# Turning round the branch to a second path, with branch hints ahead of it, at the end of an attention and feed-forward kernel

## The chip, the cores and the metric

The kernel runs on one core of one Trainium2 chip. The metric is the device time of one execution in microseconds (us). Three runs of the kernel before took 246.99, 247.65 and 247.90 us, median 247.65. A further execution was profiled: it took 247.33 us, and its span, from the first to the last instruction of the program, is 244.8 us (244.82 in the trace).

A core has five engines with a sequencer each: TensorE (PE; its weight loads are listed as PEld), VectorE (DVE), ScalarE (ACT), GpSimd (POOL) and SyncE (SP). Each runs its own list of instructions, and they wait for each other by semaphores.

## The reference

Attention in chunks of 64 rows, then a gated feed-forward layer without a nonlinearity:

```
q, k, v: (8, 8, 576, 64)            chunks of 64 along the 576
scores = q_c @ k_c^T / sqrt(64);  scores -= rowmax(scores)
attn   = exp(scores) / (rowsum + 1e-9);  a = attn @ v_c
x      = a as (4608, 512)           rows: batch and position, columns: heads
out    = ((x @ w1) * (x @ w2)) @ w3 @ w_out        w1, w2: (512, 1024), w3: (1024, 1024), w_out: (1024, 512)
```

## The kernel before

The 4608 rows are cut into 18 pieces of 256 (`p` below), two of which form a group. For each piece, GpSimd's queue loads q, k and v; VectorE transposes q and k (`do_T`); TensorE makes the scores (`do_S`), ScalarE their exponentials without subtracting the row maximum (`do_E`), TensorE the product with v and a column of ones (`do_P`), VectorE divides by the sums (`do_N`) and transposes (`do_X`). For each group and each 128 columns of the hidden layer, TensorE makes x @ w1 and x @ w2 (`do_A`, `do_B`), ScalarE copies the first out (`do_C`) and VectorE multiplies the two (`do_M`). The product w3 @ w_out is made once on the chip (`do_V`, `do_W`, `do_Z`), so that one more product per piece gives the output (`do_O`); ScalarE copies it out of PSUM (`do_Y`, line 382) and SyncE's queue stores it (`do_Q`, line 200). The last piece, `O17`, is stored in three parts, each after a copy of its own (line 375): two copies on ScalarE, the last on VectorE.

The order of all this is written out by hand in `ORDER`: a step's letter names the function, its numbers the piece and the part. Each engine executes its instructions in that order.

Since the exponentials are taken without the row maximum, their sums may leave the range in which the result can be trusted. Step `F` (`do_F`) tests the stored reciprocals of the sums and writes to `flag` how many of the 128 partitions are sound. Step `L` (`do_L`, line 428) loads `flag` into a register of each engine. It stands near the end of `ORDER`:

```
... O15 Y14 Q14 L O16 Y15 Q15 Y16 Q16 O17
```

When all steps have been issued, line 507 opens a conditional block: if fewer than 128 partitions are sound, the whole computation is done again by a second path, `do_rescue`, which subtracts the row maximum. With the inputs of the reference all partitions are sound, and the second path is not executed.

How the branch is laid out matters here. The program has these blocks: the main part, which ends with a compare-and-branch on each of the five engines; the second path; an *even-out* block, which is executed when the second path is not, and brings the semaphores to the values that they would have behind the second path (one to five semaphore instructions per engine); and the end, with the drains and a barrier of all engines (its instructions carry line 534). In the kernel before, the blocks lie in this order on each engine: main part, even-out block, second path, end. The compare-and-branch falls through into the even-out block, and the even-out block ends with a jump over the second path to the end; the profile lists both as COMPARE_BRANCH of line 507. Counted in the program, the second path is 7523 instructions long on TensorE, 281 on VectorE, 192 on ScalarE, 187 on GpSimd and 1 on SyncE; the main part has 5560, 287, 204, 149 and 139.

SyncE's part of the end waits for the landing of every store that is still under way, and then reports to the barrier like the others. GpSimd collects the reports.

Of the kernel before, what the change touches and what calls it, by code (L numbers as in the profile page):

```python
# [44 lines left out]
def kernel(  # L45
# [13 lines left out]
    P = 128  # L59
# [365 lines left out]
    whole = []  # L425

    def do_L():
        whole.append(nc.values_load(flag[:], min_val=0, max_val=P))

    def do_rescue():  # L430

# [72 lines left out]
          "W": do_W, "Z": do_Z, "O": do_O, "Y": do_Y, "Q": do_Q, "F": do_F, "L": do_L}  # L504
    for step in ORDER.split():
        do[step[0]](*(int(n) for n in step[1:].split(".") if n))
    with tc.If(whole[0] < P, preferred_fallthrough_block=False):  # L507
        do_rescue()


# [28 lines left out]
```

## Time and profile before

| what | us |
|---|---|
| median of three runs | 247.65 (246.99 to 247.90) |
| the profiled execution | 247.33 |
| its span | 244.8 |
| TensorE busy | 225.6 (92%) |
| VectorE busy | 155.4 (63%) |
| ScalarE busy | 85.0 (35%) |
| GpSimd busy | 83.2 (34%) |
| mean granted TensorE clock | 0.994 of full speed |

The page of the profile gives busy time per engine, the span in 40 slices, the DMA queues, the chain of waits that ended last, and the groups of instructions by line. Register, branch, semaphore and DMA-issuing instructions are not counted as busy; they are found by asking the trace for one line of the program. There, an engine's sequencer is written with a q (PEldq, DVEq). Among the DMA queues, the page lists two of the kind "instruction": q8 with 23 packets and 0.38 MB, so about 16 KB each, and q14 with 11 packets and 0.09 MB, about 8 KB each. These carry the engines' own instructions. The stores run on q1.

### The profile page before, as it was taken

What the parts mean: (1) busy time and instruction counts of PE and PEld (TensorE: products, weight loads), DVE (VectorE), ACT (ScalarE), POOL (GpSimd) and SP (SyncE); (2) the same over time, 40 slices, a digit from 0 to 9 for tenths busy, and PEclk for the clock granted to TensorE, in tenths of its full rate; (3) what the DMA queues carried; (4) which work ended last, traced back from release to release, by engine and by line L of the source; (5) the groups of instructions that cost most, each with busy time, mean ns of one, the idle gap of its engine ahead of it and who ended that gap; (6) DMA issues with size and microseconds to landing.
All of it is one profiled execution on the core that took longest, in us unless ns stands there. A gap on an engine that the chain in (4) does not pass through costs nothing. (4 is left out here: it accounts for less than half of the span.)

```text
span 244.8 us, 6384 instructions
## 1 busy us (share of the span) xinstructions
PE 225.6 (92%) x2731; PEld 120.1 (49%) x2753; DVE 155.4 (63%) x238; ACT 85.0 (35%) x116; POOL 83.2 (34%) x112
## 2 busy tenths in 40 slices
PE   1289989999999989999999999999999999999991
PEld 1247878864545444444444444444444444444450
DVE  1756799699799588999998899647450431242000
ACT  2412424423334335335135263243223332423240
POOL 8847876556985336754050410000000000000000
PEclk9999999999999999999999999999999999999997
DMA  7999999999999999999999794555202201200434
GB/s 178 179 185 179 185 168 202 196 192 169 163 174 226 228 210 263 185 214 198 219 209 271 161 156 115 133 153 193 64 1 90 85 0 69 105 1 0 171 122 145
DMA packets 93746, 37.71 MB, mean 154 GB/s; under 512 B 75152, under 2 KB 86672, under 8 KB 93712
## 3 DMA queue, kind: packets, MB, share of 16 engines
q0 software_dynamic: 82592, 18.88, 83.1%
q1 hardware_dynamic: 10080, 17.83, 24.1%
q10 hardware_dynamic: 1040, 0.52, 0.8%
q8 instruction: 23, 0.38, 0.6%
q14 instruction: 11, 0.09, 0.1%
HBM read 38.80 MB, written 9.44 MB: 197 GB/s over the span
## 5 line engine op out<-in xcount | busy, mean ns | idle before, releaser
L93 PE MATMUL ab_ps<-xt,w 128*128 128x512 bf16 (+1 forms) x681 | 127.0, 342 | 1.0 <-DVE xt L283 0.3
L93 PEld LDWEIGHTS <-w 128*128 128x128 bf16 x704 | 67.1, 98 | 55.4 <-issue 1.3
L352 DVE TENSOR_TENSOR ab<-a_sb,ab_ps 128x512 bf16<-128x512 f32 x71 | 47.6, 674 | 40.5 <-ACT a_sb L337 40.1
L337 ACT COPY a_sb<-ab_ps 128x512 f32<-128x512 f32 x71 | 41.6, 586 | 81.3 <-PE ab_ps L93 81.1
L93 PE MATMUL o_ps<-w3o,ab 128*128 128x512 bf16 (+1 forms) x285 | 63.3, 373 | 0.6
L208 DVE STREAM_TRANSPOSE qkT<-qk 128x1024 bf16<-128x1024 bf16 x36 | 45.0, 1287 | 7.2 <-ACT qk L143 5.6
L93 PEld LDWEIGHTS <-ab 128*128 128x128 bf16 x296 | 28.4, 98 | 32.3
L96 POOL DMA_DIRECT2D vbuf<-in_v_dram x40 | 33.9, 854 | 17.6 <-DMA qk<-in_k_dram 5.0
L382 ACT COPY o_sb<-o_ps 128x1024 f32<-128x1024 f32 x17 | 17.2, 1012 | 45.5 <-PE o_ps L93 41.3
L271 DVE TENSOR_TENSOR xn<-pv,rcs 128x512 bf16<-128x512 f32 x36 | 24.9, 691 | 1.4
L96 POOL DMA_DIRECT2D qk<-in_q_dram x23 | 18.1, 789 | 9.0 <-DVE ab L352 2.6
L96 POOL DMA_DIRECT2D qk<-in_k_dram x23 | 18.0, 786 | 8.1 <-DMA vbuf<-in_v_dram 5.3
L241 ACT ACTIVATE e<-s_ps 128x1024 bf16<-128x1024 f32 x16 | 15.9, 1028 | 1.9 <-PE s_ps L93 1.8
L93 PE MATMUL w_ps<-wo,w3T 128*128 128x512 bf16 x62 | 13.9, 379 | 0.1
L291 DVE STREAM_TRANSPOSE xm<-xn 128x512 bf16<-128x512 bf16 x20 | 13.6, 697 | 0.2
L268 DVE RECIPROCAL rcs<-pv 128x8 f32<-128x8 f32 x36 | 6.9, 193 | 10.4 <-PE pv L93 10.4
L96 POOL DMA_DIRECT2D w<-in_moe_w_dram x16 | 11.1, 696 | 5.6 <-DMA wo<-in_moe_w_out_dram 2.9
L93 PEld LDWEIGHTS <-e 64*32 64x32 bf16 (+1 forms) x832 | 7.8, 97 | 8.9 <-issue 7.1
L93 PE MATMUL pv<-vbuf,e 64*32 64x65 bf16 (+1 forms) x832 | 10.2, 198 | 1.9 <-ACT e L241 1.1
L283 DVE STREAM_TRANSPOSE xt<-xn 128x512 bf16<-128x512 bf16 x16 | 11.4, 711 | 0.5
L93 PEld LDWEIGHTS <-qkT 32*64 32x64 bf16 x512 | 5.6, 117 | 10.5 <-DVE qkT L208 8.1
L375 DVE COPY o_sb<-o_ps 128x256 f32<-128x256 f32 x1 | 0.4, 425 | 16.0 <-PEq L507 16.0
(30 smaller groups left out, 54.5 us busy)
## 6 DMA issues: line engine op xcount, KB each, us to landing
out_dram<-o_sb SPq DMA_DIRECT2D x17, 512.0 KB, 4.0
qkm<-qkT SPq DMA_DIRECT2D x40, 128.0 KB, 4.9
vbuf<-in_v_dram POOLq DMA_DIRECT2D x32, 128.0 KB, 8.5
w<-in_moe_w_dram POOLq DMA_DIRECT2D x16, 256.0 KB, 9.6
qk<-in_q_dram POOLq DMA_DIRECT2D x11, 256.0 KB, 7.1
qk<-in_k_dram POOLq DMA_DIRECT2D x11, 256.0 KB, 7.7
xt<-xm SPq DMA_DIRECT2D x40, 64.0 KB, 3.0
wo<-in_moe_w_out_dram POOLq DMA_DIRECT2D x4, 256.0 KB, 7.5
```

The lines of the kernel that those rows point to most:

```text
L93: return inorder(nc.tensor.matmul(*a, **kw))
L96: return inorder(nc.gpsimd.dma_start(dst, src))
L208: inorder(nc.vector.transpose(qkT_t[g][:, :, p % 2, s, heads(h)].rearrange("p e h (y t) -> p h t e y", t=2), qk_t[p][:, s, heads(h)].rearr ...
L241: inorder(nc.scalar.activation(e_t[p][:, :, heads(hh)], s_t[p][:].rearrange("p u (h q) -> p u h q", q=CH)[:, :, heads(hh)], Exp, scale=sca ...
L268: inorder(nc.vector.reciprocal(rc, pv[:, :, :, D:W]))
L271: inorder(nc.vector.tensor_mul(xn_t[p][:, u], pv[:, :, :, 0:D], rc.to_broadcast([P, 2, 4, D])))
L283: inorder(nc.vector.transpose(new_xt(g)[:].rearrange("p (o t) -> p o t", o=KO)[:, :, t0:t0 + UT] .rearrange("p o (m y) -> p m o y", y=BL), ...
L291: inorder(nc.vector.transpose(xm_t[g][:, u, :, m].rearrange("p o (c y) -> p c o y", y=BL), xn_t[p][:].rearrange("p u r m d -> p (u r) m d" ...
L337: inorder(nc.scalar.copy(a_t[p, j][:], ps_t[p, j][:, 0, :]))
L352: inorder(nc.vector.tensor_mul(o, view(a_t.pop((p, j))[:]), view(ps_t.pop((p, j))[:, 1, :])))
L375: inorder(copy(o_sb[:, u, n0:n1], t[:, 0, 0:n1 - n0]))
L382: inorder(nc.scalar.copy(o_sb[:], ps_t.pop(p)[:]))
```

## The change

```diff
     def do_L():
         whole.append(nc.values_load(flag[:], min_val=0, max_val=P))
+        tc.mark_branch_hint_location("whole", "LikelyTaken",
+                                     (mybir.EngineType.PE, mybir.EngineType.DVE, mybir.EngineType.Activation))
...
-    with tc.If(whole[0] < P, preferred_fallthrough_block=False):
+    with tc.If(whole[0] < P, preferred_fallthrough_block=True, label="whole"):
         do_rescue()
```

It has two parts. With `preferred_fallthrough_block=True` the compare-and-branch falls through into the second path and branches to the even-out block, which now lies behind the second path, next to the end: main part, second path, even-out block, end. The jump from the even-out block to the end is no longer needed. And on TensorE, VectorE and ScalarE a hint instruction is placed at step `L`, behind the load of the register: it names the branch with the label `whole` and says that it will likely be taken. GpSimd and SyncE get no hint. Nothing of the computation is changed or moved.

## The prediction

> **What bounds the kernel now.** I read the page first: TensorE is busy in 92% of the span, and it is still at full share in the last slices, so up to about 239.6 us the matmuls set the time and the change touches none of them. The page's chain of waits says nothing of the rest: it holds one copy.
>
> ```profile
> ## 4 chain that ended last, share of the span: by engine, by line
> DVE 0%
> DVE o_sb L375 0%
> ```
>
> That copy ends at 240.1, and the span ends at 244.8. So 4.7 us at the end hold no counted work, and only sequencer instructions can say what fills them. Next I asked for the instructions of line 507 (the branch) from 236 us on. Columns: instruction, count, shortest/median/longest duration in ns, first and last start in us.
>
> ```profile
> L507 PEldq COMPARE_BRANCH  x2: 91/2084/4077, 237.3 to 239.8; - x2
> L507 ACTq COMPARE_BRANCH  x2: 38/42/45, 238.8 to 239.2; - x2
> L507 DVEq COMPARE_BRANCH  x2: 51/53/55, 239.7 to 240.2; - x2
> L507 SPq COMPARE_BRANCH  x2: 38/46/53, 240.5 to 240.6; - x2
> ```
>
> Each engine branches twice: the test, which falls through to the even-out block, and a jump from there over the second path to the end. TensorE's jump, at 239.78, takes 4.08 us. The drains behind the jumps (line 534, from 239.6 to 244 us) show who arrives when:
>
> ```profile
> L534 ACTq DRAIN  x1: 81/81/81, 239.7 to 239.7; - x1
> L534 DVEq DRAIN  x1: 58/58/58, 243.5 to 243.5; - x1
> L534 PEldq DRAIN  x1: 75/75/75, 243.9 to 243.9; - x1
> ```
>
> ScalarE loses 0.4 us in its jump, VectorE 3.2 (240.24 to 243.48), TensorE 4.1. The DMA view of 241.3 to 241.5 us says why: a packet of the instruction queue q8 begins at 241.34 and takes 1.09 us, and a q14 packet of 8 KB begins at 241.51. The target's instructions have to be brought in.
>
> ```profile
> q1 hardware_dynamic: 36, 0.02, 38.6%
> q8 instruction: 1, 0.02, 34.2%
> ```
>
> The third thing at the end is the last store, as SyncE's waits show (total us, times, longest):
>
> ```profile
> SPq L534 <- DMA out_dram<-o_sb: 2.2, 1, 2.2
> ```
>
> It is issued at 240.13. Of its 16 semaphore increments in the trace, 15 come from 241.66 to 242.01 (median 241.74), the last at 243.57. The DMA view of 242.5 to 244 us has 8 late packets of 1 KB in it, one DMA engine's part, which start when the q8 packet ends:
>
> ```profile
> q1 hardware_dynamic: 8, 0.01, 2.4%
> ```
>
> So TensorE's fetch also holds up the last store. SyncE reports 0.21 us after the landing (243.78), TensorE at 244.00, and the two closing barrier rounds take 0.82 us from there to 244.82. The store alone would end the span at 244.6. **Only the fetch's removal from both places shortens the span.**
>
> **Part 1, turning the branch.** It removes one jump per engine: the even-out block now lies next to the end. The test becomes the far jump. TensorE's sequencer reads the test at 237.27, 2.3 us before its last matmul ends, so a stall there is partly covered: 237.36 + 4.08 = 241.4 instead of 243.9. On VectorE the test is read at 239.71, beside the copy; with a stall of 3.24, even-out (0.1) and drain it would report at 243.13 instead of 243.5. GpSimd's branch is at 181.5 and it reports with the drain of 185.0: nobody waits for it. SyncE saves one branch (0.1 us) ahead of its 2.2 us wait: nothing.
>
> **Part 2, the hints.** One instruction each on TensorE, VectorE and ScalarE behind the register load of line 428. No row shows a hint. Below: it costs no more than a branch that does not stall, 0.04 to 0.09 us. Above: its sequencer stands for a whole fetch, 4.08 us. At the load (228.6) TensorE's sequencer is about 4.1 us ahead of its array (the group it has finished handing over ends only at 232.7, where ScalarE's copy starts), so 0.5 us at most would show; VectorE is idle for 16 us there, ScalarE for 2.9 us. I take the lower end: the register load at the same place takes 0.5 us and nothing waits for it. If the hints bring the target in, TensorE reports at about 239.8 and VectorE at 240.3, and the store is late next. A hint placed 8 us ahead of TensorE's test leaves twice the 4.08 that a fetch took.
>
> **Part 3, the last store.** With no fetch on its DMA engine it lands at the median, 241.74. But each jump is followed by a fetch of the block behind the target: TensorE's starts at 244.55, 0.69 us after its jump, GpSimd's 0.63 after its drain began, VectorE's 0.62. After the change TensorE jumps at 237.36, so this fetch would start near 238.05, when the packets of the stores start (238.1). What it does to them is in the DMA views of 209.3 to 212 us, with one q8 packet, and of 226.5 to 237 us, with none (last column: us from issue to landing):
>
> ```profile
> q8 instruction: 1, 0.02, 2.2%
> ...
> out_dram<-o_sb SPq DMA_DIRECT2D x1, 512.0 KB, 4.0
> ```
>
> ```profile
> out_dram<-o_sb SPq DMA_DIRECT2D x3, 512.0 KB, 2.8
> ```
>
> One DMA engine is late by 1.2 to 1.3 us. The four stores behind each other use all engines without a pause but for some 0.4 us before the last one, so I take 1.26 - 0.4 = 0.86: landing at 242.6. Ends: 241.74 (no such fetch, or an earlier one) and 243.0 (nothing recovered). SyncE's 0.21 and the rounds' 0.82 follow: span 243.63, between 242.77 and 244.03. **Gain 1.19, between 0.79 and 2.05.**
>
> **Part 4, behind the span.** The profiled run took 247.33, 2.51 more than its span. The trace keeps the updates of the barrier semaphore behind it: 245.06, 245.09, 245.30, then nothing until 246.06. VectorE's following block starts at 244.10 and takes 0.47, and its earlier fetch took 1.5 us from its end to the next instruction: 246.07. I read the gap as VectorE waiting for this block; jumping at 239.8 it has it long before. Gain 0.72 (246.06 - 245.30 less a step of 0.04). Ends: 0, and 1.5 if a second gap (246.30 to 247.09) is TensorE's following block (244.55 + 1.10 + 1.42 = 247.07).
>
> **Sum** against the profiled run: 247.33 - 1.19 - 0.72 = 245.42. That run lies 0.32 below the median of 247.65, within the spread of the three (246.99 to 247.90); I put the forecast at **245.5**.
>
> [...] The profile shows no fetch ahead of a jump, only the one behind it. [...]
>
> **Rivals.** (a) *The hints do nothing.* For it: no row shows one working. VectorE reports at 243.13, the span ends at 243.95 (-0.87), and its following block comes at 243.57 + 0.47 + 1.5 = 245.54 instead of 246.06: 0.52 in all, 246.8. Price against mine 1.4. (b) *No fetch meets the last store,* because the following block comes in with the hint: gain 2.05 + 0.72 to 1.5, so 243.8 to 244.6. Against it: all three jumps that fetched were followed by another. (c) *Span gain alone,* the barrier gap having another cause: 246.1 to 246.5. (d) *Slower:* the hinted block takes the place of one that TensorE still needs, so that it fetches between hint and branch, on its critical path, and once more for what that fetch displaced. Two fetches are 8.16 less the lead of 4.1: +4.1 on the last matmul, less the 1.9 of my forecast: 249.5. It decides only from the second fetch on, since one fits in the lead. Against it: the DMA view of 212 to 239.5 us has no packet of q8, so TensorE crosses no block there. (e) *Nothing changes:* the second path is still jumped over by a late branch, 247.3.
>
> **How the numbers follow.** My case 0.42 (own range 244.4 to 246.3), (b) 0.20, (a) 0.15, (c) 0.08, (e) 0.06, (d) 0.09. About 0.5% (1.24 us, so 246.4) is what can be told from no change. Faster: my case, (b), most of (c): 0.69. Same: (a), (e), the rest of (c): 0.22. Slower: 0.09. The range leaves out (d), half of (e) and the far end of (b): 244.0 to 247.0.
>
> **What would show it.** One COMPARE_BRANCH per engine, all under 0.1 us on TensorE and VectorE; VectorE's drain near 240.3; q8 and q14 packets between 223 and 235 us, which are absent now on q8; a q8 packet near 238; the wait for out_dram down from 2.2 to about 1.2 us; no gap behind 245.3's counterpart. I am wrong if TensorE's branch still takes 4 us, if q8 shows a packet between hint and branch with matmuls standing still, or if the last store lands as late as now.

## The result

The changed kernel takes 246.00 us (median of 9 runs, 245.83 to 247.15), the kernel before 247.54 (9 runs): ratio 0.9946, 95% interval 0.9926 to 0.9966. Measured again (e11 below), the ratio was 0.9941 (0.9916 to 0.9967). The profiled executions give 245.90 against 247.33. Of these 1.43 us, 0.72 lie in the span (244.82 to 244.10) and 0.71 behind it (2.51 to 1.80 us).

Line 507 of before is line 509 in the changed kernel, line 534 is 536. The branch now (instruction, count, shortest/median/longest ns, first and last start in us):

```profile
L509 PEldq COMPARE_BRANCH  x1: 398/398/398, 237.9 to 237.9; - x1
L509 ACTq COMPARE_BRANCH  x1: 68/68/68, 239.6 to 239.6; - x1
L509 DVEq COMPARE_BRANCH  x1: 90/90/90, 240.7 to 240.7; - x1
```

One branch per engine and no stall: TensorE's takes 0.4 us where its jump took 4.08. The drains of the changed kernel between 239 and 243.35 us:

```profile
L536 PEldq DRAIN  x1: 8/8/8, 239.8 to 239.8; - x1
L536 ACTq DRAIN  x1: 8/8/8, 240.2 to 240.2; - x1
L536 DVEq DRAIN  x1: 17/17/17, 241.4 to 241.4; - x1
```

TensorE arrives 4.1 us and VectorE 2.1 us earlier than before. Yet the span is only 0.72 us shorter, since the last store, issued at 240.17, still lands at 243.07 (before: 243.57). SyncE's waits (total us, times, longest) show it as what is late next:

```profile
SPq L536 <- DMA out_dram<-o_sb: 1.7, 3, 1.2
```

The cause, which e4 below confirms, is in the DMA view of 239.5 to 240.2 us (queue, packets, MB, share of 16 engines): a packet of the instruction queue q8, which I take for TensorE's following block (TensorE's branch ends at 238.30), starts at 239.93 in the midst of the stores and takes 0.99 us.

```profile
q1 hardware_dynamic: 144, 0.26, 99.3%
q8 instruction: 1, 0.02, 8.8%
```

The last four stores land at 240.31, 242.44, 242.75 and 243.07, while 14 or 15 of the 16 increments of each come by 240.05, 240.71, 241.09 and 241.86. One DMA engine's part is 1.73 us late in the second store, and 1.2 to 1.3 us in the last.

Behind the span, the third update of the closing barrier's semaphore is at 244.58 and the fourth at 244.62: the gap of 0.76 us that before has there (245.30 to 246.06) is gone.

Two things happened that the diff does not say. The hints are not issued at step `L`. Line 536, in the first 2 us:

```profile
L536 ACTq BRANCH_PREFETCH_HINT  x1: 45/45/45, 0.7 to 0.7; - x1
L536 DVEq BRANCH_PREFETCH_HINT  x1: 51/51/51, 0.8 to 0.8; - x1
L536 PEldq BRANCH_PREFETCH_HINT  x1: 50/50/50, 0.8 to 0.8; - x1
```

I read this so: a hint's row names no tile, nothing held it to its place, and the scheduler put it first. In e5, where the hints are tied to step `L`, they stand at 223.0 to 229.3 us. And the register loads of the three hinted engines went to the end of the main part (before: 228.6, 229.3 and 223.0 us):

```profile
L428 PEldq TENSOR_LOAD <-flag x1: 488/488/488, 237.3 to 237.3; - x1
L428 ACTq TENSOR_LOAD <-flag x1: 752/752/752, 238.8 to 238.8; - x1
L428 DVEq TENSOR_LOAD <-flag x1: 817/817/817, 239.8 to 239.8; - x1
```

In e3, where the hint is written ahead of the load, the loads stay at step `L` (228.4, 229.0 and 222.7 us).

### The profile page after: what moved, and what is told of

Its sections match the earlier page's. It is cut to its first block, busy times and chain, and to the rows that moved or that the text cites. A ratio compares the mean times of both kernels' runs of the same rounds, so it can differ in the third digit from the quotient of the medians.

```text
span 244.1 us, 6404 instructions
## 1 busy us (share of the span) xinstructions
PE 227.4 (93%) x2753; PEld 120.2 (49%) x2753; DVE 155.2 (64%) x238; ACT 85.2 (35%) x116; POOL 83.3 (34%) x112
```

## The experiments

My theory at the start was the prediction's: the hints bring the targets in, the last store held up by TensorE's following block sets the end, and VectorE's early jump closes the gap in the barrier. The rival was that one half of the change alone, or the moved loads, explains the time. The main part ends up to 0.9 us earlier or later from profile to profile, so the last columns count from the issue of the last store. "Reports" is the start of the drain. "Step" is the time from the third to the fourth barrier update behind the span. What the columns leave out: in e1, e3, e5 and e9 SyncE issues the last store itself late, by 0.22, 0.45, 0.07 and 0.09 us (see the last section).

| kernel | median us | ratio to before (95%) | TensorE's stalling branch, us | VectorE reports | last store lands | span ends | step |
|---|---|---|---|---|---|---|---|
| before | 247.5 | 1 | 4.08 | +3.35 | +3.44 | +4.69 | 0.76 |
| changed | 246.00 | 0.9946 (0.9926-0.9966) | 0.40 | +1.20 | +2.90 | +3.93 | 0.04 |
| e1 turn only | 246.84 | 0.9980 (0.9966-0.9993) | 4.22 | +2.50 | +2.93 | +3.95 | 0.55 |
| e2 hints only | 247.82 | 1.0024 (1.0004-1.0045) | 3.82 | +3.95 | +3.17 | +6.46 | 1.35 |
| e3 loads early | 246.34 | 0.9959 (0.9946-0.9973) | 0.40 | -0.16 | +2.93 | +3.96 | 0.04 |
| e4 late jump | 245.46 | 0.9919 (0.9897-0.9941) | 0.39 | +1.35 | +1.88 | +2.91 | 0.04 |
| e5 hints at L | 246.23 | 0.9958 (0.9938-0.9978) | 0.40 | +2.75 | +2.94 | +3.97 | 0.04 |
| e6 VectorE's hint | 245.98 | 0.9942 (0.9920-0.9963) | 3.88 | +0.92 | +2.83 | +3.86 | 0.04 |
| e7 TensorE's hint | 246.18 | 0.9949 (0.9928-0.9969) | 0.39 | +3.04 | +2.97 | +4.03 | 0.04 |
| e8 no second path | 245.02 | 0.9893 (0.9873-0.9914) | none | - | +1.70 | +2.71 | 0.04 |
| e9 ScalarE's hint | 246.31 | 0.9941 (0.9920-0.9963) | 4.02 | +2.52 | +2.94 | +3.97 | 0.04 |
| e10 late, loads early | 245.12 | 0.9892 (0.9868-0.9916) | 0.39 | +0.73 | +1.93 | +2.96 | 0.04 |
| e11 changed again | 246.30 | 0.9941 (0.9916-0.9967) | 0.40 | +1.20 | +2.99 | +4.02 | 0.04 |
| e12 late, ScalarE's hint | 247.19 | 0.9994 (0.9979-1.0009) | 3.54 | +3.24 | +2.73 | +5.01 | 0.04 |

**e1, the turn alone.**

```diff
-        tc.mark_branch_hint_location("whole", "LikelyTaken",
-                                     (mybir.EngineType.PE, mybir.EngineType.DVE, mybir.EngineType.Activation))
...
-    with tc.If(whole[0] < P, preferred_fallthrough_block=True, label="whole"):
+    with tc.If(whole[0] < P, preferred_fallthrough_block=True):
```

> The changed kernel without its hints: the branch is turned, nothing else. Theory (the hints bring the target in, and the turn alone only starts the fetch earlier): TensorE's test takes about 4 us from 237.3 and VectorE about 3.2 us from 239.7, VectorE reports near 243.1 and its following block comes near 245.5; 246.8 us, 0.7 to 0.8 above the changed kernel. Rival (the hints do nothing, the turn is the whole gain): no stall of 4 us, and the changed kernel's time, 246.0 us.

Measured 246.84 us, a fall of 0.2% (0.07 to 0.34). Line 507 in it:

```profile
L507 PEldq COMPARE_BRANCH  x1: 4215/4215/4215, 237.4 to 237.4; - x1
...
L507 DVEq COMPARE_BRANCH  x1: 72/72/72, 239.8 to 239.8; - x1
...
L507 DVEq EVENT_SEMAPHORE  x1: 21/21/21, 242.9 to 242.9; - x1
```

Both stalls are there (VectorE's 3.1 us lie between its branch and the even-out semaphore), and so is a gap of 0.55 us in the barrier. VectorE reports at 243.0, where 243.13 was worked out. The theory holds: without hints the change is worth less than half.

**e2, the hints alone.** The changed kernel with `preferred_fallthrough_block=False`.

> The kernel before with the hints and the label, the branch not turned. Theory: the hinted branch is the test, which falls through; the jump that stalls has no hint, so TensorE's second branch still takes 4 us; the time of before, 247.5 us, or up to 0.5 above it, because the register loads now stand just ahead of the branch on VectorE. Rival (the hints alone bring the gain): near 246.0 us.

Measured 247.82 us, 0.24% above before (0.04 to 0.45). TensorE's second branch stalls 3.82 us; the hinted one is the test, which falls through. VectorE, its load late, reports last, and its last instruction of the program waits until 246.5 (line 536, from 243 to 247 us):

```profile
L536 DVEq EVENT_SEMAPHORE  x2: 21/21/21, 244.2 to 246.5; - x2
```

No other engine has an instruction of the program after 244.8. A q14 packet of 8 KB starts at 244.60 and takes 0.51; VectorE's instruction follows 1.4 us behind its end, as its drain in before follows 1.5 us behind the end of the packet of 241.51. I read this as VectorE waiting for its following block here, one instruction ahead of the barrier behind the span, and in before, where VectorE has no hint and so one instruction less, in that barrier. So I took VectorE for the gap's owner.

**e3, the loads back at step L.** The call of the hint is put ahead of the load in `do_L`.

```diff
+        tc.mark_branch_hint_location("whole", "LikelyTaken", ...)
         whole.append(nc.values_load(flag[:], min_val=0, max_val=P))
-        tc.mark_branch_hint_location("whole", "LikelyTaken", ...)
```

> The changed kernel with the hint traced ahead of the register load instead of behind it, so that the loads of the three engines stand at step L again and not just ahead of the branch. Theory (the end is set by the last store, held up by the fetch that follows TensorE's jump): TensorE jumps 0.6 us and VectorE 0.9 us earlier, but the fetch still falls into the stores; 245.8 us, within 0.3 of the changed kernel. Rival (the late loads eat the missing gain): 0.6 to 0.9 us below the changed kernel, 245.2 us.

Measured 246.34 us: the late loads did not eat the missing gain. TensorE jumps at 237.0, a q8 packet starts at 238.29 and takes 1.56 us, and all of the last four stores are late on one DMA engine (landing 5.0 us after issue in the first). Then something that I had not expected: line 200 on SyncE, the issues of the last two stores (from 238.8 to 240.5 us):

```profile
L200 SPq DMA_DIRECT2D out_dram<-o_sb x2: 516/926/1337, 238.9 to 240.3; - x2
```

An issue that takes 0.33 to 0.37 us in before takes 1.34 here, so the last store itself is issued about 0.45 us late, for all 16 engines.

**e4, TensorE's jump held until VectorE's last copy.** VectorE copies one element of the last output behind its last copy, and TensorE's sequencer waits for that ahead of its load and branch (`o_last`, set where the last output is made, holds its tile).

```diff
...
+    ticked = consts.tile([1, 1], mybir.dt.int32, name="ticked")
+    inorder(nc.vector.tensor_copy(ticked[:], o_last[0][0:1, 1, DM - 1:DM]))
+    ins, late = nc.values_load_multi_w_load_instructions(ticked[:], engines=(mybir.EngineType.PE,))
+    inorder(ins[0])
     with tc.If(whole[0] < P, preferred_fallthrough_block=True, label="whole"):
```

> The changed kernel with TensorE's sequencer held ahead of its register load and branch until VectorE's last copy is done (a one-element copy by VectorE behind its last, on which TensorE waits). Theory: TensorE's following fetch then starts after the last store's packets; no store is late by over 0.5 us, the last lands near 241.8 to 242.3; the span falls to 243.0 to 243.4, and the time by 0.4 to 1.0 us to 245.0 to 245.6. Rival (the late store has another cause): the last store lands near 243.1 as before and the time is 246.0 us or more, though TensorE jumps 3 us later.

Measured 245.46 us, 0.5 below the changed kernel's 246.00, though TensorE jumps 0.9 us behind the issue of the last store (241.9) and not 2.3 us ahead of it. The DMA view of 238 to 242 us now has no q8 packet (it starts at 243.09), and the stores land in the 2.8 and 2.1 us that they take undisturbed:

```profile
q1 hardware_dynamic: 604, 0.96, 66.0%
q14 instruction: 1, 0.01, 0.7%
issues: line engine op xcount, KB each, median us to landing
out_dram<-o_sb SPq DMA_DIRECT2D x1, 512.0 KB, 2.8
out_dram<-o_sb SPq DMA_DIRECT2D x1, 256.0 KB, 2.1
```

The last store lands 1.88 us after its issue instead of 2.90. So the q8 packet that comes behind TensorE's jump was what held it up; in e12 below one starts among the stores again (241.66), and the last store lands 2.73 us after its issue.

**e5, each hint tied to step L.**

```diff
+        for e in (mybir.EngineType.PE, mybir.EngineType.DVE, mybir.EngineType.Activation):
+            ahead = next(i for i in reversed(nc.cur_bb.bb.instructions)
+                         if i.engine == e and "Load" not in type(i).__name__)
+            with tc.issue_after(ahead):
+                tc.mark_branch_hint_location("whole", "LikelyTaken", (e,))
         whole.append(nc.values_load(flag[:], min_val=0, max_val=P))
-        tc.mark_branch_hint_location("whole", "LikelyTaken", ...)
```

> The changed kernel with each hint tied behind the instruction that precedes step L on its engine, so that it is issued at L (near 223 us on VectorE, 228 on TensorE, 229 on ScalarE) and not in the first microsecond; the loads stand at L too, as in e3. Theory (a hint works from wherever it is, if a fetch fits in ahead of the branch): a q8 packet of its own near 229 to 232 us, TensorE's branch under 0.5 us, the time of e3, 246.3 us. Rival (the hint must be known when the engine enters the branch's block near 210 us, since only then is the next block chosen): TensorE stalls 4 us as without hints, 246.8 us.

Measured 246.23 us. TensorE's hint, at 228.7, is followed by a q8 packet of its own at 230.44 (DMA view of 229 to 232 us):

```profile
q8 instruction: 1, 0.02, 2.0%
```

and its branch takes 0.4 us. VectorE's hint, at 223.0, has no effect: no q14 packet starts between 220 and 240.4 us, and between branch and even-out it stalls 3.1 us again:

```profile
L512 DVEq COMPARE_BRANCH  x1: 90/90/90, 239.8 to 239.8; - x1
...
L512 DVEq EVENT_SEMAPHORE  x1: 21/21/21, 242.9 to 242.9; - x1
```

And yet the barrier has no gap, though VectorE reports as late as in e1. That contradicts part 4 of the prediction.

**e6, VectorE's hint alone.** The tuple of engines in the hint is cut to `(mybir.EngineType.DVE,)`.

> The changed kernel with VectorE's hint alone. Theory (VectorE's arrival and its following block are what the hints buy; TensorE's stall is covered by the early test): TensorE stalls 4 us from 237.3 and reports near 241.7, which nobody waits for; the last store lands near 243.3 as in e1 and e3; no gap in the barrier behind the span; 246.2 to 246.4 us. Rival (TensorE's hint makes the gain): 246.8 us or more.

Measured 245.98 us, as the changed kernel. TensorE's stall of 3.88 us is hidden: it reports at 241.6, ahead of the last store's landing, 2.83 us after its issue (near 243.2).

**e7, TensorE's hint alone.** The tuple is cut to `(mybir.EngineType.PE,)`.

> The changed kernel with TensorE's hint alone. Theory: VectorE's test stalls 3.2 us and it reports near 243.1; its following block comes near 245.5, so the gap in the barrier behind the span is back; 246.6 to 246.8 us. Rival (TensorE's hint makes the gain): 246.0 us.

Measured 246.18 us: my theory fell. VectorE has no hint, stalls as in e1 (239.5 to 242.9) and reports near 243.0; a q14 packet starts at 243.50, as in e1. Still the barrier's step is 0.04 and not 0.55. VectorE is late with the gap (e1) and without it (here), so an early arrival cannot be what closes the gap here.

The step is 0.04 in every turned kernel so far that has a hint on any engine (the changed kernel, e3 to e7), 0.55 in e1, turned without a hint, and 1.35 in e2, hinted but not turned. So the new theory was: in a turned kernel a hint on any engine closes the gap, whether or not that engine stalls, and whether or not VectorE arrives early.

**e8, no second path.** The conditional block and the hint are left out.

> The kernel without the conditional block: the second path, its branch, its even-out blocks and the register loads of four engines are left out, so that no engine jumps at the end. It shows what the branch costs in all. Theory: no instruction block is fetched among the last stores, the last store lands 1.6 us after its issue (near 241.8), the span ends near 242.9, and nothing waits in the barrier behind it: 244.8 to 245.1 us, 2.5 us below the kernel before and within 0.6 of the kernel with the late jump. Rival (the drains and the barrier cost this much anyway): 246 us.

Measured 245.02 us. This is what the branch costs in all: 1.1% (0.9 to 1.3) of the kernel before. No instruction packet starts from 221 us on, and the last store lands 1.70 us after its issue.

**e9, ScalarE's hint alone.** The tuple is cut to `(mybir.EngineType.Activation,)`. ScalarE lost only 0.4 us in its jump before, so no engine that stalls is hinted.

> The changed kernel with ScalarE's hint alone. ScalarE never waited for its jump's target, so no engine that stalls is hinted. [...] Rival, the prediction's part 4 (the early jump of VectorE closes the gap): the gap of 0.55 us is back as in e1, 246.8 us.

Measured 246.31 us, beside 246.30 of the changed kernel on the same chip (e11); 246.0 to 246.4 was put down for the new theory, with both stalls and no gap. Line 509:

```profile
L509 PEldq COMPARE_BRANCH  x1: 4015/4015/4015, 238.1 to 238.1; - x1
...
L509 DVEq COMPARE_BRANCH  x1: 72/72/72, 240.5 to 240.5; - x1
...
L509 DVEq EVENT_SEMAPHORE  x1: 21/21/21, 243.4 to 243.4; - x1
```

Both stalls are back, 4.0 and 2.9 us, the gap is not, and the time is that of three hints. The rival, with the gap back, falls, and the new theory holds as far as it was tested: what the hints bring the changed kernel comes with a hint on any engine, and not with the end of TensorE's or VectorE's stall. The span's gain comes with the turn: counted from the last store's issue it ends at 3.97 us here, at 3.95 without hints (e1) and at 3.93 with all three, against 4.69 before.

How a hint on another engine closes the gap, no view shows. One more thing in the traces goes with it: behind the gap of before, e1 and e2 one more q14 packet starts (246.53, 245.94 and 247.17 us, 0.44 to 0.47 behind the fourth update), and no kernel without the gap has a packet there.

**e10, e4 with the loads early.** The edits of e3 and e4 together.

> The kernel of e4 (TensorE's sequencer held until VectorE's last copy) with the register loads at step L as in e3, so that TensorE jumps 0.5 us earlier than in e4, and ScalarE and VectorE 0.5 to 0.9 us earlier. Theory (the last store is late only where a fetch meets it): TensorE's fetch still follows the last store's packets; 245.0 to 245.5 us, as e4 or up to 0.3 below. Rival (VectorE's or ScalarE's fetch now meets the last store as well): 0.3 us or more above e4, 245.8 us.

Measured 245.12 us, ratio 0.9892, the same as without any second path (0.9893). Its median is the lowest here of those that keep the second path, but it is not told apart from e4: the intervals overlap, and the end is no shorter (+2.96 against +2.91).

**e11, the changed kernel again.**

> The changed kernel as it is, on the same chip as e9 and e10, for a direct comparison. Both theories: 246.0 us, within 0.3.

Measured 246.30 us.

**e12, e4 with ScalarE's hint alone.**

TensorE and VectorE have no hint here: what is TensorE's worth where the jump is late?

> [...] Theory (the hint on TensorE did bring its target in, and this pays only where the jump has no cover): TensorE's branch takes 4 us from about 241, it reports near 245.1, the span ends near 245.9; 247.3 to 248.0 us, 2 us above e4. Rival (the hints bring nothing in at all): as e4 and e10, 245.1 to 245.5 us.

Measured 247.19 us, 1.7 above e4. Line 516, the branch:

```profile
L516 PEldq COMPARE_BRANCH  x1: 3538/3538/3538, 240.7 to 240.7; - x1
```

In e4, with a hint on TensorE, it takes 0.39 us. So the hint does take TensorE's stall away, and it pays where the jump has no cover. In the changed kernel it has cover: e6, without TensorE's hint, takes 245.98 us against 246.00. A q8 packet that starts at 241.66, during the stall, meets the last store, which lands 2.73 us after its issue instead of the 1.88 of e4.

## Why the prediction was right, and where its steps failed

The time (246.0) lies in the range, the likeliest case came, and the forecast of 245.5 was 0.5 too low. That it came so near is in part luck: one half of the gain came by a way that the prediction did not have (parts 2 and 4).

- **Part 1** held. With the turn alone TensorE's stalled branch lets it report at 241.8 (worked out: 241.4) and VectorE at 243.0 (243.13), and the time is 246.84, against 246.8 worked out for rival (a). But rival (a) let the last store land in time, with the span ending at 243.95; in e1 a q8 packet that starts during the stall, at 238.35, met the stores, the last one landed at 243.42 and the span ended at 244.45. What came as worked out is the end of VectorE's gap: 245.48, against 245.54.
- **Part 2** was right that a hint costs nothing that shows (0.05 us each) and that the stalls go. It was wrong on where things stand: the hints are in the first microsecond and the loads just ahead of the branch, so the q8 packet looked for between 223 and 235 us is absent, and VectorE's drain is at 241.4 instead of 240.3. VectorE reports about 0.9 us later than it could, which the last store covers: e3 has the loads early and is no faster. And the worth of TensorE's hint was overrated: e6 and e9 run with TensorE stalling 3.9 to 4.0 us in the changed kernel's time. "Only the fetch's removal from both places shortens the span" was too strong: with the branch turned, the stall lies under TensorE's last matmuls and the last store (in e6 it begins at 237.5 and TensorE reports at 241.6).
- **Part 3** had the mechanism, shown by e4, but a term was too small. "I take 1.26 - 0.4 = 0.86" became 1.73 - 0.4 = 1.3: the fetch held up the engine that it met by 1.73 us, not the 1.26 of the one row that I had, and 0.4 was recovered as assumed. The store landed at 243.07 instead of 242.6, the last 0.21 and 0.82 came as worked out, and the span gained 0.72 instead of 1.19, just outside the near end of 0.79. The fetch also came at 239.93 and not near 238.05, since the branch ended 0.9 us later than I had it (238.30) and the fetch started 1.6 us behind it instead of 0.7. This hardly mattered: in e3 it came at 238.29, met the stores too, and the time was 246.34.
- **Part 4** had the size, 0.71 measured against 0.72, and, as I read e2, the owner, VectorE, but "jumping at 239.8 it has it long before" is not what it takes. In e5, e7 and e9 VectorE is late and the gap is gone all the same. A hint on another engine closes it without an early jump (step 0.04 in e7 and e9), so that the size came out is luck. Whether an early jump alone would have closed it stays open, since in no turned kernel without a hint is VectorE early. The second gap that I kept as a far end (0.79 us, 246.30 to 247.09) is still there in the changed kernel (244.86 to 245.65), though the q8 packet behind TensorE's jump ended at 240.92, and in e8, where no engine jumps (244.37 to 245.16): it is not TensorE's.
- **Rival (a)**, that the hints do nothing, falls. With a hint at `L`, e5 has a q8 packet at 230.44 that no other kernel has, and TensorE's branch takes 0.4 us; without one on TensorE the stalling branch takes 3.5 to 4.2. And e1, without hints, is 0.84 us above the changed kernel (246.84 against 246.00).

## What to carry to other kernels

When the time at the end is in no engine's busy time, list the sequencers' branches and drains, and the instruction queues among the DMA packets: a far jump that stalled cost TensorE 3.5 to 4.2 us and VectorE 2.9 to 3.4 here, and TensorE's cost again through the store that a q8 packet met (the last one landed 2.73 us after its issue in e12, 1.88 in e4). The hint on TensorE took away only the first (a branch of 0.4 us); a q8 packet still followed the jump (239.93 in the changed kernel), so the hinted jump was better held until VectorE's last copy, which was worth 0.5 to 1.2 us here (e4 and e10 against the changed kernel), beside 0.5 to 0.7 for the turn (e1 against before, by ratio and by median) and 0.5 to 0.9 for a hint on any engine (e1 against the other turned kernels without a late jump). After an edit that adds an instruction without operands, look where the scheduler put it, and what moved with it.

## What the runs showed of the hardware that I had not expected

- A q8 packet among the stores goes with a slower issue of the next ones. In e1, e3, e5, e6 and e9 a q8 packet starts 0.6 to 0.95 us ahead of the issue of the last store but one, and this issue takes 0.75 to 1.34 us; in all other kernels here it takes 0.34 to 0.35. In e3 and e1, where it is longest (1.34 and 1.11), the last store is issued 0.45 and 0.22 us late, and so comes late on all 16 DMA engines. Whether and how the packet slows the issue, no view shows.
- TensorE's hint got a packet of its own where it was given 8.6 us ahead of the branch (e5, 230.44). Given in the first microsecond it adds none: the changed kernel has 21 q8 packets before the branch, as before has, and TensorE does not stall. What the hint brings in there, and when, no view shows.
- VectorE's hint 16.7 us and six instructions ahead of its branch did nothing (e5), while the one in the first microsecond worked (VectorE's even-out 0.6 us behind its branch instead of 3.1). Why, no run here shows.
